# Seven gate and value groups ahead of a q transpose in TensorE's queue of a retention-plus-SwiGLU kernel

## The chip, the cores and the metric

The kernel runs on one core of a Trainium2 chip. A core has TensorE (matrix products, written to PSUM), VectorE, ScalarE and GpSimd, and SyncE, which only issues transfers; GpSimd issues transfers too, beside its own arithmetic. The metric is the device time of one execution in microseconds (us); lower is better. In the profile PE is TensorE's matmuls, PEld its weight loads, DVE is VectorE, ACT is ScalarE, POOL is GpSimd and SP is SyncE.

## What is computed

```python
def _attn_ref(q, k, v):                       # q, k, v: 4 x 8 x 768 x 64
    gamma = 1.0 - 2.0 ** (-5.0 - np.arange(H))
    for t in range(S):
        state = gamma * state + einsum('bhd,bhe->bhde', k[:, :, t], v[:, :, t])
        y[:, :, t] = scale * einsum('bhd,bhde->bhe', q[:, :, t], state)

def _moe_ref(x, w_gate, w_val, w_out, rms_g): # x: 3072 tokens x 512
    xn = x / sqrt(mean(x * x) + 1e-06) * rms_g
    g = xn @ w_gate                           # 512 x 1536
    return (g * sigmoid(g) * (xn @ w_val)) @ w_out
```

The first part is a linear attention with a decay per head; its output, token by token, goes through an RMS norm and a gated feed-forward network.

## The kernel before

**How the work is cut.** The 768 positions are cut into 6 chunks (c, 0 to 5) of 128, and there are 4 batches (b, 0 to 3), so a chunk has 4 x 128 = 512 tokens. Per chunk and batch the attention part transposes q and k, multiplies k with q to scores, masks the scores, multiplies them with v and adds the contribution of the state. Then come the norm, a transpose of the normed rows, and the feed-forward part, which works on the whole chunk: 12 blocks (n, 0 to 11) of 128 hidden columns for the gate and for the value. The output product, and in chunk 5 the gate and value products as well, are done with 7 products of sums and differences of quarters in place of 8; those sums are the z operations.

**What sets the order.** The order is written out by hand in a table, `ORDER` (lines 17 to 105), one word for each operation. A loop at the end (lines 784 to 788) takes the words one after the other and calls the function of that name; each engine runs what it is given strictly in that order, and waits where an operand or a buffer isn't ready:

```python
for w in ORDER.split():
    w, _, bk = w.partition("/")
    w, _, en = w.partition("@")
    f, *a = w.split(".")
    F[f](ENG.get(en), [int(i) for i in bk], *map(int, a))
```

A word is the operation's name, its numbers, after `@` the engine (D, A, P or S for VectorE, ScalarE, GpSimd or SyncE), and after `/` the PSUM banks that its result goes to. `g.0.4.6.3.4/4` is the gate product of chunk 0, blocks 4 to 5, batch 3, in bank 4. There are 8 banks, each with one buffer: a new result in a bank waits until the last reader of the former one is done. So the digit behind `/` orders engines too.

**The words that are spoken of:**

- `Lq`, `Lk`, `Lv` (line 329): load of q, k or v of chunk.batch; `wg`, `wv` (line 338) and `wo` (line 345): load of weight columns. On GpSimd's queue they convert to bf16 on the way; the tiles are `qb`, `kb`, `vp`, `wg_b`, `wv_b`, `wo_b`.
- `Tq`, `Tk` (line 386): transpose of q or k on TensorE into PSUM (`t_ps`), 4 matmuls. `Eq` (lines 395 and 152) and `Ek` copy the result to `qT` and `kT`. From chunk 2 on, `tq` and `tk` (line 402) do the transposes by DMA on SyncE's queue.
- `A` (line 418): scores (`a_ps`); `M0`, `M1` (line 441): masking on VectorE; `Y` (lines 456 and 460): scores times v, plus q times the state (`y_ps`).
- `K` (line 541), `U` (line 549), `B` (line 556): the state's update, its sum on VectorE, and on GpSimd the state in bf16 (`st_b`); `D` (line 532): k times its decay.
- `S` (line 473), `R` (lines 483 and 485), `N` (line 497): the row's sum of squares on ScalarE, `ms` and `rstd` on GpSimd (two instructions of 128x1), and the normed row `xn` on VectorE. `X` (line 510) transposes it, `XE` (line 152) copies it to `xnT`.
- `g`, `v` (line 564): gate and value product, 4 matmuls for each block; `s` (line 574): SiLU of the gate on ScalarE; `h` (line 586): its product with the value on VectorE, into `hT`.
- `z1` to `z4` (line 633): the sums of quarters of `hT` for the 7 products; `a1`, `b2`, `c5` and so on (line 660): those products.
- in chunk 5 `ga..`, `gb..`, `gc..`, `va..` and so on (line 750): its gate and value products; `gq`, `vq` (line 152) keep a part of them in SBUF (`sn`), `gr`, `vr` (line 762) add the parts, `gs` (line 772) is the SiLU.

A gate product of 4 matmuls reads the normed rows of the batches that its last two numbers span, so `g.0.4.6.3.4` needs batch 3 of chunk 0 only, `g.0.5.6.0.3` batches 0 to 2:

```python
for n in range(n0, n1):
    for s in range(KS):
        nc.tensor.matmul(p[:, (n - n0) * m:(n - n0 + 1) * m], W[w][0][:, s, n * 128:(n + 1) * 128],
                         xnT[c][:, s, b0 * C:b1 * C], start=s == 0, stop=s == KS - 1)
```

Of the kernel before, what the change touches and what calls it, by code (L numbers as in the profile page):

```python
# [23 lines left out]
K.0.2/2 S.0.3 s.0.0.2.0.1 N.0.1 U.0.2@A wg.4.6 X.0.2/5 R.0.3 XE.0.2@D D.0.1@D v.0.0.2.0.1/6 X.0.1/1 wv.4.6 causal
XE.0.1@A Lk.1.2@P v.0.0.2.2.3/4 h.0.0.2.0.1 g.0.0.2.2.3/2 D.0.3@D g.0.0.2.1.2/5 g.0.2.3.0.3/7 s.0.0.2.2.3 h.0.0.2.2.3
s.0.0.2.1.2 g.0.3.4.0.3/1 N.0.3 v.0.0.2.1.2/6 D.1.1@D s.0.3.4.0.3 Lq.1.2@P K.0.1/3 Tk.1.1/2 Ek.1.1@D K.0.3/5 X.0.3/4
h.0.0.2.1.2 Tq.1.2/0 Eq.1.2@D wg.6.9 v.0.3.4.0.3/1 Tq.1.1/2 Lk.1.3@P XE.0.3@A g.0.0.4.3.4/6 s.0.2.3.0.3 v.0.2.3.0.3/4
v.0.5.6.0.3/7 Eq.1.1@D Lq.1.3@P U.0.1@A U.0.3@A h.0.2.3.0.3 wv.6.9 g.0.5.6.0.3/3 s.0.5.6.0.3 g.0.4.5.0.3/5 Tk.1.2/2
h.0.3.4.0.3 h.0.5.6.0.3 v.0.4.5.0.3/4 Tk.1.3/0 v.0.4.6.3.4/1 v.0.0.4.3.4/3 s.0.4.5.0.3 h.0.4.5.0.3 Ek.1.2@A A.1.2/75
s.0.0.4.3.4 h.0.0.4.3.4 Ek.1.3@A g.0.7.8.0.4/2 s.0.7.8.0.4 g.0.4.6.3.4/4 s.0.4.6.3.4 Tq.1.3/6 g.0.6.7.0.4/0 mc.0@P  # L30
g.0.8.9.0.4/3 s.0.8.9.0.4 Lq.1.0@P mc.1@P Lk.1.0@P M0.1.2 Lv.1.3@P Eq.1.3@D h.0.4.6.3.4 Tq.1.0/7 M1.1.2 Eq.1.0@D
# [787 lines left out]
```

## Time and profile before

| | us |
|---|---|
| three runs | 232.84, 234.69, 234.11 (median 234.11) |
| the profiled execution, its own time | 233.33 |
| its span, first to last instruction | 231.6 (1.7 lies around it) |
| PE busy | 219.7 |
| DVE, POOL, ACT busy | 178.0, 151.0, 100.1 |

The profile shows one execution. A row of its timeline reads: start in us from the span's start, duration in us, engine, line, operation, out<-in, shapes, how many instructions; in square brackets how long the engine was idle before it, and what ended that. `PEclk` and the granted clock are the share of TensorE's full clock that it was given. Matmuls are pipelined: a group's next one starts before the last one's end is shown, so starts are compared with starts.

### The profile page before, as it was taken

To read this page: it belongs to the slowest core of one execution; us is meant where nothing else is said; L and a number is where in the kernel's file an instruction comes from. 1 tells how busy PE (TensorE), PEld (TensorE's weight loads), DVE (VectorE), ACT (ScalarE), POOL (GpSimd) and SP (SyncE) were. 2 spreads that over 40 slices of the span, in tenths; PEclk is the share of its full clock that TensorE was granted. 3 is DMA by queue.
4 is the path that set the end of the run, shared out by engine and by line. 5 is a ranking of instruction groups with operands and counts; after the bars stand their busy time and mean duration, and the time that the engine had idled before them with its cause. 6 is when DMAs were issued, how large, how long until landed. Compare 5 with 4: busy or idle time off the path is not lost.

```text
span 231.6 us, 5477 instructions
## 1 busy us (share of the span) xinstructions
PE 219.7 (95%) x2100; PEld 147.0 (63%) x2119; DVE 178.0 (77%) x328; ACT 100.1 (43%) x222; POOL 151.0 (65%) x207
## 2 busy tenths in 40 slices
PE   8999299999999999999999999999999999999992
PEld 3568177566445796446765446787446678888871
DVE  6598136986498978869768888889889589999931
ACT  7875224364436441332702454425442536863220
POOL 8969999738906862837814980377269789477700
PEclk9999889999999999999999999999999999999999
DMA  7999999998289967769758966955957353000243
GB/s 135 156 182 135 160 174 179 207 185 199 57 159 165 209 126 173 127 133 212 153 128 216 224 148 130 203 147 142 264 112 180 25 159 136 3 0 3 90 165 110
DMA packets 108172, 33.65 MB, mean 145 GB/s; under 512 B 94449, under 2 KB 108145, under 8 KB 108146
## 3 DMA queue, kind: packets, MB, share of 16 engines
q1 hardware_dynamic: 84674, 25.70, 49.3%
q0 software_dynamic: 23472, 7.60, 30.1%
q8 instruction: 16, 0.26, 0.5%
q14 instruction: 10, 0.08, 0.1%
HBM read 28.31 MB, written 6.29 MB: 149 GB/s over the span
## 4 chain that ended last, share of the span: by engine, by line
PE 85%; DMA 5%; POOL 4%; DVE 2%; issue 2%; ACT 1%; POOLq 0%; DVEq 0%
PE v_ps L564 22%; PE g_ps L564 21%; PE a L660 13%; PE c L660 7%; PE b L660 3%; DMA qb<-in_q_dram 2%; PE ga L750 2%; PE va L750 2%; DMA kb<-in_k_dram 2%; PE a_ps L418 2%; PE y_ps L456 2%; PE y_ps L460 2%; PE kv_ps L541 1%; PE vc L750 1%; PE gc L750 1%
## 5 line engine op out<-in xcount | busy, mean ns | idle before, releaser
L574 ACT ACTIVATE sg<-g_ps 128x512 bf16<-128x512 f32 (+2 forms) x64 | 35.5, 570 | 64.8 <-PE g_ps L564 52.4
L564 PE MATMUL v_ps<-xnT,wv_b 128*128 128x512 bf16 (+2 forms) x287 | 58.7, 340 | 0.6 <-issue 0.2
L564 PE MATMUL g_ps<-xnT,wg_b 128*128 128x512 bf16 (+2 forms) x286 | 57.9, 341 | 0.5
L586 DVE TENSOR_TENSOR hT<-sg,v_ps 128x512 bf16<-128x512 bf16 (+2 forms) x64 | 40.7, 649 | 15.8 <-PE v_ps L564 11.5
L564 PEld LDWEIGHTS <-wv_b 128*128 128x128 bf16 x296 | 26.0, 98 | 23.0 <-issue 0.3
L564 PEld LDWEIGHTS <-wg_b 128*128 128x128 bf16 x296 | 26.2, 100 | 22.3
L660 PEld LDWEIGHTS <-hT 128*128 128x128 bf16 x288 | 27.6, 98 | 4.6 <-issue 0.6
L633 POOL TENSOR_TENSOR z<-hT 128x512 bf16<-128x512 bf16 x10 | 12.3, 1234 | 19.1 <-DVE hT L586 18.9
L660 PEld LDWEIGHTS <-z 128*128 128x128 bf16 x216 | 20.6, 98 | 4.0 <-issue 0.7
L473 ACT ACTIVATE xsq<-y_ps 128x512 bf16<-128x512 f32 x22 | 13.2, 599 | 20.4 <-PE y_ps L460 17.3
L633 POOL TENSOR_TENSOR hT<-hT 128x512 bf16<-128x512 bf16 x12 | 15.2, 1265 | 10.1 <-DVE z L633 5.3
L441 DVE TENSOR_TENSOR am<-a_ps,causal 128x512 bf16<-128x512 f32 x32 | 20.1, 682 | 1.6 <-PE a_ps L418 1.4
L497 DVE SCALAR_TENSOR_TENSOR xn<-y_ps,rstd,g_bc 128x512 bf16<-128x512 f32 x22 | 16.4, 748 | 6.1 <-POOL rstd L485 6.1
L556 POOL CAST st_b<-st_f 64x256 bf16<-64x256 f32 x40 | 17.4, 434 | 1.9 <-DVE st_f L549 0.6
L660 PE MATMUL a<-wo_b,hT 128*128 128x256 bf16 x144 | 18.0, 273 | 0.0
L152 ACT COPY sn<-a 128x512 f32<-128x512 f32 x15 | 8.8, 586 | 15.4 <-PE a L660 13.1
L485 POOL TENSOR_TENSOR rstd<-ms,mhalf 128x1 f32<-128x1 f32 x24 | 13.2, 552 | 2.0
L683 DVE TENSOR_TENSOR r<-c,sn 128x512 f32<-128x512 f32 (+1 forms) x13 | 8.4, 647 | 7.1 <-PE c L660 4.4
L633 POOL TENSOR_TENSOR z<-z,hT 128x512 bf16<-128x512 bf16 x9 | 10.6, 1179 | 4.5 <-DVE z L633 3.1
L483 POOL TENSOR_SCALAR ms<-ssq 128x1 f32<-128x1 f32 x24 | 4.5, 189 | 12.8 <-ACT xsq L473 11.8
L549 DVE TENSOR_TENSOR st_f<-st_f,kv_ps 128x256 f32<-128x256 f32 x16 | 6.5, 416 | 5.0 <-PE kv_ps L541 5.0
L441 DVE TENSOR_TENSOR am<-a_ps,mask 128x512 bf16<-128x512 f32 x16 | 10.3, 683 | 0.0
(159 smaller groups left out, 393.8 us busy)
## 6 DMA issues: line engine op xcount, KB each, us to landing
out_dram<-r SPq DMA_DIRECT2D x22, 256.0 KB, 2.4
kf<-in_k_dram SPq DMA_DIRECT2D x18, 256.0 KB, 3.9
qf<-in_q_dram SPq DMA_DIRECT2D x16, 256.0 KB, 4.2
vf<-in_v_dram SPq DMA_DIRECT2D x16, 256.0 KB, 4.1
wo_b<-in_moe_w_out_dram POOLq DMA_DIRECT2D x3, 512.0 KB, 11.6
qb<-in_q_dram POOLq DMA_DIRECT2D x8, 128.0 KB, 5.3
vp<-in_v_dram POOLq DMA_DIRECT2D x8, 128.0 KB, 6.4
kb<-in_k_dram POOLq DMA_DIRECT2D x6, 128.0 KB, 5.3
```

The lines of the kernel that those rows point to most:

```text
L152: (e.copy if e is ACT else e.tensor_copy)(out, in_)
L441: DVE.tensor_tensor(out=u["am"][:, i], in0=u["a"][i], in1=m, op=ALU.mult)
L473: ACT.activation(xsq, flat(u["y"]), AF.Square, accum_out=u["ssq"])
L485: POOL.tensor_tensor(out=u["rstd"], in0=ms, in1=mhalf, op=ALU.pow)
L497: DVE.scalar_tensor_tensor(out=u["xn"], in0=flat(u["y"]), scalar=u["rstd"], in1=g_bc, op0=ALU.mult, op1=ALU.mult)
L556: POOL.tensor_copy(st_b[b][r, :, i * 64:i * 64 + 64], st_f[b][r])
L564: nc.tensor.matmul(p[:, (n - n0) * m:(n - n0 + 1) * m], W[w][0][:, s, n * 128:(n + 1) * 128], xnT[c][:, s, b0 * C:b1 * C], start=s == 0, s ...
L574: ACT.activation(sg[:, :cols], done["wg", c, n0, b0][:, :cols], AF.Silu)
L586: DVE.tensor_tensor(out=h_of(c, r)[:, i:i + n1 - n0, b0 * C:b1 * C], in0=sg, in1=p, op=ALU.mult)
L633: e.tensor_tensor(out=x, in0=a, in1=b, op=how)
L660: nc.tensor.matmul(done[x, c][:, q], left(i, c, r)[:, k, q * C:q * C + C], right(i)[:, r, k], start=first and q == r == k == 0, stop=r == ...
L750: nc.tensor.matmul(p[:, q], l[:, r, q], m[:, k], start=first and q == k == 0, stop=q == k == 1, skip_group_check=True)
```

## The change

Nothing is computed otherwise: the table holds the same 1065 words. What changes is where some stand, and the bank digits of most words that have one. Two lines of the table (before and after):

```diff
-h.0.0.2.1.2 Tq.1.2/0 Eq.1.2@D wg.6.9 v.0.3.4.0.3/1 Tq.1.1/2 Lk.1.3@P XE.0.3@A g.0.0.4.3.4/6 s.0.2.3.0.3 v.0.2.3.0.3/4
+K.0.3/7 X.0.3/5 h.0.0.2.1.2 wg.6.9 v.0.3.4.0.3/2 Tq.1.1/4 Lk.1.3@P XE.0.3@A g.0.0.4.3.4/0 g.0.4.6.3.4/3 v.0.2.3.0.3/1
```

**TensorE, end of chunk 0.** These rows are TensorE's from the transpose of batch 3's normed rows on (`xt_ps`); of each group of like matmuls the first is shown. Before, `t_ps_677` is `Tq.1.2`, the q transpose of chunk 1, batch 2, and `t_ps_690` is `Tq.1.1`:

```order
L510 MATMUL xt_ps_671<-ident_94,xn_629 128x128
L386 MATMUL t_ps_677<-ident_94,qb_644 128x128
L564 MATMUL v_ps_685<-xnT_496,wv_b_134 128x384
L386 MATMUL t_ps_690<-ident_94,qb_414 128x128
L564 MATMUL g_ps_698<-xnT_496,wg_b_133 128x128
L564 MATMUL v_ps_717<-xnT_496,wv_b_134 128x384
L564 MATMUL v_ps_722<-xnT_496,wv_b_134 128x384
L564 MATMUL g_ps_735<-xnT_496,wg_b_133 128x384
L564 MATMUL g_ps_742<-xnT_496,wg_b_133 128x384
L386 MATMUL t_ps_747<-ident_94,kb_581 128x128
L564 MATMUL v_ps_755<-xnT_496,wv_b_134 128x384
```

The same place after, where `t_ps_743` is `Tq.1.2`, `t_ps_685` is `Tq.1.1`, and `g_ps_710` is `g.0.4.6.3.4`:

```order
L510 MATMUL xt_ps_673<-ident_94,xn_629 128x128
L564 MATMUL v_ps_680<-xnT_496,wv_b_134 128x384
L386 MATMUL t_ps_685<-ident_94,qb_414 128x128
L564 MATMUL g_ps_693<-xnT_496,wg_b_133 128x128
L564 MATMUL g_ps_710<-xnT_496,wg_b_133 128x128
L564 MATMUL v_ps_719<-xnT_496,wv_b_134 128x384
L564 MATMUL v_ps_724<-xnT_496,wv_b_134 128x384
L564 MATMUL g_ps_730<-xnT_496,wg_b_133 128x384
L564 MATMUL g_ps_736<-xnT_496,wg_b_133 128x384
L386 MATMUL t_ps_743<-ident_94,qb_646 128x128
L386 MATMUL t_ps_757<-ident_94,kb_581 128x128
```

`Tq.1.2` moved from the first place behind `X.0.3` to behind seven gate and value groups and `Tq.1.1`; six of those seven already stood next to it, and `g.0.4.6.3.4` comes up from behind the first scores of chunk 1 (`A.1.2`). A little further on `Tk.1.3` moves behind `v.0.4.6.3.4` and `v.0.0.4.3.4`. ScalarE's and VectorE's copies and products follow: `s.0.2.3.0.3` goes ahead of the copy `XE.0.3`, and on VectorE `h.0.3.4.0.3` and `h.0.2.3.0.3` go ahead of `Eq.1.1` and `Eq.1.2`. GpSimd's loads stay as they were.

**GpSimd, chunk 1.** One piece of the difference of GpSimd's queue; the kd rows ahead of it are `D.1.0` and `D.1.2`, z is `z1.0.0`, st_b_127 is the state of batch 2 (`B.0.2`), and the first ms and rstd rows are `R.1.3`:

```order
 L532 TENSOR_TENSOR kd<-kb,vdec 128x512 x2
-L633 TENSOR_TENSOR z<-hT 128x512
-L556 CAST st_b_127<-st_f_123 64x4x64 x2
 L483 TENSOR_SCALAR ms<-ssq 128x1
 L485 TENSOR_TENSOR rstd<-ms,mhalf 128x1
+L556 CAST st_b_127<-st_f_123 64x4x64 x2
+L633 TENSOR_TENSOR z<-hT 128x512
```

`R.1.3` moves ahead of `B.0.2` and `z1.0.0`, and these two change places; `R.1.1`, `R.1.0` and `R.1.2` follow behind as before.

**VectorE, chunk 5.** TensorE's order in chunk 5 is unchanged, VectorE's and ScalarE's is not. VectorE before, from `gr3.5.1` (vf_3528) on; `vf_3546` is `vr2.5.1`, z_3576 is `z1.4.0`, `vf_3582` is `gr3.5.0`, and the row that reads `va_3438` is `h.5.6.8.0.2`:

```order
L762 TENSOR_TENSOR vf_3528<-gc_3481,sn_3405 128x512
L762 TENSOR_TENSOR vf_3546<-vc_3533,sn_3544 128x512
L586 TENSOR_TENSOR hT_3522<-kb_3505,vf_3546 128x2x256
L633 TENSOR_TENSOR z_3576<-hT_3250 128x512
L762 TENSOR_TENSOR vf_3582<-gc_3515,sn_3496 128x512
L586 TENSOR_TENSOR hT_3522<-kb_3511,va_3438 128x2x256
L762 TENSOR_TENSOR vf_3604<-vc_3533,sn_3502 128x512
```

And after, with `vr2.5.1` as vf_3585 and `gr3.5.0` as vf_3592:

```order
L762 TENSOR_TENSOR vf_3528<-gc_3481,sn_3405 128x512
L633 TENSOR_TENSOR z_3567<-hT_3250 128x512
L586 TENSOR_TENSOR hT_3520<-kb_3522,va_3438 128x2x256
L762 TENSOR_TENSOR vf_3585<-vc_3531,sn_3542 128x512
L586 TENSOR_TENSOR hT_3520<-kb_3505,vf_3585 128x2x256
L762 TENSOR_TENSOR vf_3592<-gc_3513,sn_3496 128x512
L762 TENSOR_TENSOR vf_3626<-vc_3531,sn_3502 128x512
```

`h.5.6.8.0.2` moves ahead of three operations that stood before it, and `vr3.5.1` (vf_3604, now vf_3626) stays behind `gr3.5.0`.

**Banks.** Of the 255 words that take banks, 108 now follow another word in their bank than before. Two that are used below: `Tk.1.2` (t_ps_757) now follows `Tq.1.2` in bank 4, and `vb2.5.2` in chunk 5 now follows `va1.5.1` in bank 3, the accumulator that `h.5.6.8.0.2` reads last.

More of the change, by code (lines that the diff above doesn't have):

```diff
@@ L94 @@
-gq7.5.0@D gc5.5.0/5 gr2.5.0 h.5.4.6.0.2 gc3.5.1 gr3.5.1 gs2.5.0 s4.3@S vc5.5.1/7 vS3.0@P vS3.1@P va7.5.1 vq7.5.1@A
-vr2.5.1 h.5.6.8.2.4 va6.5.0 vq6.5.0@A ga4.5.0 gs4.5.0 a1.4.0.3/1 gq6.5.2@A z1.4.0@D gc3.5.0 gr3.5.0 va4.5.1 va1.5.2/4
-gs3.5.1 h.5.6.8.0.2 vq1.5.2@A vS4.0@P vc3.5.1 vr3.5.1 z2.4.0@P h.5.4.6.2.4 vb2.5.2/3 gs3.5.0 va7.5.0 vq7.5.0@A
-vc5.5.0/5 ga7.5.2 va6.5.2 vr2.5.0 vr1.5.2 gc5.5.2/6 gq7.5.2@A gr2.5.2 q1.4@A z4.4.1@P vq6.5.2@A h.5.8.10.0.2
-b2.4.0.3/7 vc3.5.0 ga4.5.2 h.5.2.4.2.4 gc3.5.2 vr3.5.0 gs2.5.2 s3.3@S s2.3@S z1.5.1@D z3.4.2@P va4.5.0 va7.5.2
@@ L99 @@
[L99 to L103 removed]
+Ek.0.1@A Ek.0.2@D yd Lk.0.3@P H.1/4 Tq.0.2/3 tab Lq.0.3@P Eq.0.2@D hot.2/6 A.0.0/7502 M0.0.0 G/1 M1.0.0 Tq.0.3/4
@@ new lines @@
+gr1.5.1 ga6.5.1 gq6.5.1@D va1.5.0/4 gq1.5.0@A gb2.5.0/6 gr1.5.0 gs1.5.1 ga1.5.2/7 gq1.5.2@A gS3.0@P vq1.5.0@D
+gb2.5.2/0 va1.5.1/3 gs1.5.0 vq1.5.1@A gr1.5.2 vb2.5.0/5 gs1.5.2 z2.4.2@P vr1.5.0 ga7.5.1 ga6.5.0 vb2.5.1/6 h.5.0.2.0.2
+ga6.5.2 vr1.5.1 gc5.5.1/0 X4.5@P va6.5.1 gq7.5.1@A gr2.5.1 gq6.5.0@A ga7.5.0 vq6.5.1@A s2.2@S gs2.5.1 ga4.5.1
+gq7.5.0@D gc5.5.0/5 gr2.5.0 h.5.4.6.0.2 gs4.5.1 gc3.5.1 gr3.5.1 s4.3@S vc5.5.1/6 vS3.0@P vS3.1@P va7.5.1 vq7.5.1@A
+va6.5.0 vq6.5.0@A ga4.5.0 a1.4.0.3/2 z1.4.0@D gc3.5.0 va4.5.1 va1.5.2/0 h.5.6.8.0.2 gs2.5.0 vr2.5.1 h.5.6.8.2.4
@@ new lines @@
+gs4.5.0 gq6.5.2@A gr3.5.0 vq1.5.2@A vS4.0@P vc3.5.1 z2.4.0@P vb2.5.2/3 va7.5.0 vc5.5.0/1 ga7.5.2 va6.5.2 vr3.5.1
+vq7.5.0@A vr2.5.0 gc5.5.2/5 gq7.5.2@A z4.4.1@P b2.4.0.3/6 vc3.5.0 ga4.5.2 h.5.2.4.2.4 gs3.5.1 h.5.4.6.2.4 gs3.5.0
+vr1.5.2 gr2.5.2 q1.4@A vq6.5.2@A h.5.8.10.0.2 gc3.5.2 vr3.5.0 gs2.5.2 s3.3@S s2.3@S z1.5.1@D z3.4.2@P va4.5.0 va7.5.2
+h.5.0.2.2.4 z4.4.0@P z1.5.0@P z2.5.0@P z4.4.2@P h.5.2.4.0.2 vc5.5.2/3 gr3.5.2 a6.4.0.3 a1.5.0.2/1 z3.4.0@D vq7.5.2@A
+vr2.5.2 h.5.10.12.2.4 s2.1@S va4.5.2 z3.5.0@P q6.4@A gs4.5.2 h.5.10.12.0.2 b2.5.0.2/4 gs3.5.2 a1.5.2.3 vc3.5.2
```

148 lines of the change are left out of this document (71 added, 77 removed).

## The prediction

> **What bounds the kernel now.** I read first the page, then TensorE's waits, its timeline about the longest of them, and the granted clock there. The page says that TensorE is nearly always busy, except in two of the early slices:
>
> ```profile
> span 231.6 us, 5477 instructions
> PE   8999299999999999999999999999999999999992
> PEclk9999889999999999999999999999999999999999
> ```
>
> TensorE's longest wait over the whole span (us in total, times, longest); the next one is 1.1 us at the start:
>
> ```profile
> PE t_ps L386 <- DMA qb<-in_q_dram: 4.2, 1, 4.2
> ```
>
> TensorE's timeline there: the transpose that waits is `Tq.1.2`, behind `X.0.3`, and the groups that follow it are `v.0.3.4.0.3`, `Tq.1.1` and `g.0.0.4.3.4`; the last two rows, `Tq.1.0` and `Tk.1.0`, are used further on.
>
> ```profile
> 22.86 0.40 PE L510 MATMUL xt_ps<-ident,xn 128*128 128x128 bf16 x4
> 27.47 0.61 PE L386 MATMUL t_ps<-ident,qb 128*128 128x128 bf16 x4 [4.21 <-DMA qb<-in_q_dram]
> 27.87 1.49 PE L564 MATMUL v_ps<-xnT,wv_b 128*128 128x384 bf16 x4
> 29.15 0.63 PE L386 MATMUL t_ps<-ident,qb 128*128 128x128 bf16 x4
> 29.57 1.61 PE L564 MATMUL g_ps<-xnT,wg_b 128*128 128x128 bf16 x16
> ...
> 39.76 0.39 PE L386 MATMUL t_ps<-ident,qb 128*128 128x128 bf16 x4
> 39.98 0.39 PE L386 MATMUL t_ps<-ident,kb 128*128 128x128 bf16 x4
> ```
>
> In windows cut at the clock's steps (us, then busy time of PE, PEld, DVE, ACT, POOL, each with its count, then the granted clock) the idle stretch is followed by 3.41 us at half clock. The last row, of the long stretch behind, says that TensorE is then busy for 191.5 of 193.0 us: whatever comes earlier at 31 us should come earlier at the end too.
>
> ```profile
> 23.90:27.32 3.42, 0.00 (x0) 0.00 (x0) 0.00 (x0) 0.92 (x3) 3.42 (x5) 1.00 1.78 156
> 27.32:30.73 3.41, 3.26 (x23) 2.59 (x24) 1.38 (x2) 0.00 (x0) 3.39 (x4) 0.50 1.81 171
> ...
> 31.00:224.00 193.00, 191.51 (x1725) 128.55 (x1742) 157.23 (x264) 81.26 (x177) 122.93 (x158) 1.00 0.72 144
> ```
>
> **The change part by part.**
>
> *The q transpose behind seven groups.* The wait of 4.21 us ends because TensorE now has work: `v.0.3.4.0.3` can start when the transposes of 22.86 have been issued. The half clock goes with it: the 3.26 us of work in that window are 1.63 us at full clock. Together 5.84 us, the gross gain, if nothing else is late.
>
> What is late next is the queue of GpSimd's loads. Its order and its issues don't change, so I take its landings as fixed. Three rows for the walk that follows: eight matmuls of 384 columns at full clock in the chain (start, us), ScalarE's copy `XE.0.3`, and VectorE's copy `Eq.1.2`:
>
> ```profile
> 32.49 1.30 PE g_ps L564 x8
> ...
> 23.30 0.58 ACT L152 COPY xnT<-xt_ps 128x512 bf16<-128x512 bf16 x1 [1.10 <-PE xt_ps L510]
> ...
> 28.11 0.69 DVE L395 TENSOR_TENSOR qT<-t_ps,qdec 128x512 bf16<-128x512 bf16 x1 [4.64 <-PE t_ps L386]
> ```
>
> So a group of 4 x 384 columns takes 0.65, and by its columns one of 16 x 128 takes 0.87 and four transposes 0.22. Counted from 23.1 at full clock: `v.0.3.4.0.3` to 23.75, `Tq.1.1` to 24.0, `g.0.0.4.3.4` (its rows are copied to `xnT` by 23.9) to 24.8, `g.0.4.6.3.4` to 25.3, the four groups of 0.65 to 27.9. Only then comes `Tq.1.2`, whose q landed at 27.42: no wait. `Tk.1.2` now uses the same bank, so it waits for the copy `Eq.1.2`, 0.69 us on VectorE: to about 29.0, some 0.75 us of TensorE. From there the groups go on to 34.5, where `Tq.1.0` needs a q and then `Tk.1.0` a k. These two loads, GpSimd's issues with their time to landing:
>
> ```profile
> L329 POOL DMA_DIRECT2D qb<-in_q_dram x1: 955/955/955, 27.2 to 27.2; - x1
> DMA to landing us min/median/max: 7.8/7.8/7.8
> ...
> L329 POOL DMA_DIRECT2D kb<-in_k_dram x1: 948/948/948, 29.1 to 29.1; - x1
> DMA to landing us min/median/max: 6.7/6.7/6.7
> ```
>
> They land at 27.18 + 7.76 = 34.94 and 29.14 + 6.70 = 35.84 (the rows round the first digits away). So `Tk.1.0` starts at 35.9 instead of 39.98: a lead of 4.1 us. Of the gross 5.84 about 1.75 go to these waits, the 0.75 at the bank among them.
>
> *GpSimd's row sum ahead of the gate sum.* GpSimd's own rows, and the two of TensorE that wait for its results (`Y.1.2`'s second half, which needs `B.0.2`, and `X.1.1` with `X.1.0`):
>
> ```profile
> 40.27 2.04 POOL L532 TENSOR_TENSOR kd<-kb,vdec 128x512 bf16<-128x512 bf16 x2
> 42.27 1.14 POOL L633 TENSOR_TENSOR z<-hT 128x512 bf16<-128x512 bf16 x1
> 43.37 0.84 POOL L556 CAST st_b<-st_f 64x256 bf16<-64x256 f32 x2
> 45.46 0.19 POOL L483 TENSOR_SCALAR ms<-ssq 128x1 f32<-128x1 f32 x1 [1.25 <-ACT xsq L473]
> 45.73 0.56 POOL L485 TENSOR_TENSOR rstd<-ms,mhalf 128x1 f32<-128x1 f32 x1
> ...
> 48.05 0.39 PE L460 MATMUL y_ps<-st_b,qT 128*128 128x128 bf16 x4
> ...
> 51.09 0.61 PE L510 MATMUL xt_ps<-ident,xn 128*128 128x128 bf16 x8
> ```
>
> GpSimd doesn't wait for anything up to 42.27, so it can't come earlier there. With TensorE 4.1 us ahead the sum of squares for `R.1.3` is ready by 41.4 and GpSimd starts it at 42.27: 0.83 for `R.1.3`, 0.84 for `B.0.2` (to 43.95; `Y.1.2`'s second half starts there instead of at 48.05), 1.1 for `z1.0.0`, twice 0.8 for `R.1.1` and `R.1.0` (to 46.6), then the normed row, 0.75 on VectorE, to 47.35. `X.1.0` starts there instead of at 51.31 (0.22 behind 51.09): the lead is 3.95. So this part caps the lead, and takes 0.15 more. If `z1.0.0` had stayed first, `R.1.3` would have come 1.1 later, the gain of the move; with no lead the move is worth nothing, since GpSimd waited anyway.
>
> *VectorE's and ScalarE's order in chunk 5.* VectorE's and TensorE's rows of before (`vr2.5.1`, `h.5.6.8.0.2`; `va4.5.1`, `vb2.5.2`; then the transfer of the lag, `z2.5.2` on GpSimd and `a6.5.2.3` on TensorE):
>
> ```profile
> 200.37 0.68 DVE L762 TENSOR_TENSOR vf<-vc,sn 128x512 f32<-128x512 f32 x1
> 202.63 0.68 DVE L586 TENSOR_TENSOR hT<-kb,va 128x512 bf16<-128x512 bf16 x1
> ...
> 201.73 0.60 PE L750 MATMUL va<-qb,wv_b 128*128 128x256 bf16 x4
> 203.04 0.60 PE L750 MATMUL vb<-xnT,wv_b 128*128 128x256 bf16 x4
> ...
> 216.46 1.15 POOL L633 TENSOR_TENSOR z<-z,hT 128x512 bf16<-128x512 bf16 x1 [1.18 <-PE c L660]
> 217.89 0.60 PE L660 MATMUL a<-w,z 128*128 128x256 bf16 x4
> ```
>
> `h.5.6.8.0.2` needs `va4.5.1`, whose end is 201.73 + 0.60 = 202.33. VectorE does `z1.4.0` at 200.4 and then idles to 202.35, where before it did three other operations: 1.6 us of idle. It frees bank 3 at 203.0, just as `vb2.5.2` wants it. Behind it VectorE is 1.1 us late at 209 and, having had waits of its own, some 0.5 late at 216. `z2.5.2` then ends at 217.6 + 0.5, and `a6.5.2.3` waits 0.2. The bounds are 0 (cover holds) and 1.6 (the whole idle time passes to the end); I take 0.2, the row that is nearest, since TensorE's other needs there (banks 1, 5 and 6) are met 0.2 us or more ahead.
>
> *Banks.* For each of the 108 new neighbours I looked for when the last reader was done in the rows of before: none is late except where the order has moved as well, which the walk above contains. I set 0, with 0.2 either way for the least distances.
>
> *Loads of chunk 2.* SyncE's first loads wait for weights to land and don't move. The load of the q that GpSimd scales first (`Cq.2.0`), the time to landing of the loads of q about it, and GpSimd's scaling:
>
> ```profile
> 49.63 1.40 SPq L329 DMA_DIRECT2D qf<-in_q_dram  x1
> ...
> DMA to landing us min/median/max: 3.4/4.0/4.3
> ...
> 59.70 1.04 POOL L354 TENSOR_TENSOR qb<-qf,ydec 128x512 bf16<-128x512 f32 x1
> ```
>
> It is there by 49.63 + 4.3 = 53.9 and is wanted at 59.7, or at 55.75 with the lead: 1.8 us of cover remain.
>
> **The sum**, for the profiled execution: 233.33 - 4.21 - 1.63 + 1.75 + 0.15 + 0.2 = 229.6. That execution was 0.78 below the median of the three runs; from 234.11 the same 3.74 us give 230.4. I predict 230.2, between the two and nearer to the median.
>
> **Rivals.**
>
> *The half clock isn't in the timed runs.* An idle stretch of 4.2 us and a clock that steps each 3.41 us: here a whole step, 23.90 to 27.32, was empty. Were the steps shifted by more than 0.8 us against the kernel, no step would be empty. Then before has no 1.63 to lose, and the gain is 3.74 - 1.63 = 2.1: 232.0. For it: only one profiled execution shows the clock. Against: it isn't slower than the others, and a lone execution without the cost should have been below 232. [...]
>
> *GpSimd is slowed by VectorE's earlier work.* VectorE was idle from 23.5 to 28.1, while GpSimd issued loads; now it works there. If each VectorE operation kept GpSimd waiting, the 3.8 us of work that comes under GpSimd's busy stretch would delay its whole chain by up to 3.8, and with it `X.1.0`: 234.0, no change. GpSimd's issues of two loads of weights speak against it, with the window of the first beside them (VectorE, the third pair, busy for 0.76; in the second's, within 23.90 to 27.32 above, for nothing):
>
> ```profile
> 20.10 0.81 POOL L338 DMA_DIRECT2D wv_b<-in_moe_w_val_dram  x1
> 25.42 0.80 POOL L338 DMA_DIRECT2D wv_b<-in_moe_w_val_dram  x1
> ...
> 20.10:20.91 0.81, 0.81 (x10) 0.55 (x8) 0.76 (x3) 0.63 (x2) 0.81 (x2) 1.00 0.92 101
> ```
>
> The issue takes 0.81 with VectorE busy and 0.80 with it idle. [...]
>
> *The wait only moves.* TensorE meets the next load. If the loads from 30 us on landed 2 us later than in this trace, the lead at `Tk.1.0` would be 2.1: 232.2; 4 us later, nothing would be left: 234. The queue's evenness speaks against it (34.94, 35.84).
>
> *The tail takes it.* All of VectorE's 1.6 us pass to the end: 231.6.
>
> *Slower.* The new waits (0.75, 0.5, 0.7) keep the clock down: each window of 3.41 us at half clock costs 1.7. TensorE has 1.9 us of slack to `Tk.1.0`, so it takes four such windows in a row, 6.8, before the lead is gone (34.0 + 6.8 against 39.98): then some 235.0. The clock stayed at 1.00 in all windows without an idle stretch of their own length, which speaks against it.
>
> **How the numbers follow.** The forecast has 0.70; the clock rival 0.10, GpSimd's lock 0.03, the moved wait 0.06, the tail 0.07, slower 0.04. A measurement of this kernel tells about 1% from no change, 231.8 and 236.5 here. Faster: 0.70, half of the clock's and the tail's, together 0.79. Same: the rest of these, the lock, the moved wait and a quarter of slower, whose 235.0 is within 1% until a fifth window adds 1.7: 0.18. Slower 0.03. The forecast's own range is 229.2 (no cost in the tail, from the profiled execution, 4.1 of gain) to 231.4; with the scatter of the runs below and the clock and tail rivals above, 228.9 to 232.5.
>
> **What would show it.** Right: no wait of TensorE over 1 us before 30; the granted clock at 1.00 from 23.9 to 31; `Tk.1.0` at 35.9 waiting for its load; GpSimd's `R.1.3` at 42.3 without a wait; `X.1.0` at 47.4; VectorE idle for 1.6 us before `h.5.6.8.0.2`; span near 227.9. Wrong: `Tk.1.0` later than 36.5 (the loads or GpSimd's issues are later), a window at half clock, or TensorE idle in chunk 5.

## The result, and the profile after

The changed kernel takes 235.20 us (median of 20 runs, 233.73 to 236.41), the kernel before 234.13 (median of 20, 232.51 to 237.05). The ratio is 1.0054, with a 95% interval of 1.0029 to 1.0079: half a per cent slower, where 230.2 had been forecast. Ratios, here and below, leave out executions over 1.5% above the fastest of their kernel, such as the 237.05, so they differ a little from the quotient of the medians. The profiled execution took 235.53 us itself. Its page, the three lines that answer to those of before (span, TensorE's busy tenths in 40 slices, its clock):

```profile
span 233.8 us, 5480 instructions
PE   7999899999998999999999999999999999769992
PEclk9999999999999999999999999999999999988998
```

The light slice near the start, the fifth, is gone, as forecast. There are two others now, the 35th and 36th (199 to 210 us), and the clock is down in the 36th and 37th (205 to 216 us). So the gain arrives early and is lost late.

**Early, the walk holds but for its last step.** TensorE's timeline from `X.0.3` on (start, us, and in brackets the idle time ahead):

```profile
22.33 0.40 PE L510 MATMUL xt_ps<-ident,xn 128*128 128x128 bf16 x4
22.57 0.81 PE L564 MATMUL v_ps<-xnT,wv_b 128*128 128x384 bf16 x4
...
27.38 0.39 PE L386 MATMUL t_ps<-ident,qb 128*128 128x128 bf16 x4
28.55 0.38 PE L386 MATMUL t_ps<-ident,kb 128*128 128x128 bf16 x4 [0.78 <-DVE qT L395]
...
34.97 0.40 PE L386 MATMUL t_ps<-ident,kb 128*128 128x128 bf16 x4 [0.35 <-DMA kb<-in_k_dram]
```

`Tq.1.2` (27.38) doesn't wait. `Tk.1.2` waits 0.78 for the bank, and `Tk.1.0` starts at 34.97 behind its load, where it started at 39.98. This execution runs some 0.5 us ahead before the change of order begins (`X.0.3` at 22.33 against 22.86), so 4.5 of the 5.0 us belong to the change. The 0.5 is luck: the same three matmuls (`hot_ps`) take 0.81 us at 4.83 here and 1.49 us at 5.00 in before's profiled execution, and another execution of the same program (e7 below) has `X.0.3` at 22.91. GpSimd's `R.1.3` follows without a wait, and TensorE's `Y.1.2` (second half) and `X.1.0`:

```profile
41.77 0.19 POOL L483 TENSOR_SCALAR ms<-ssq 128x1 f32<-128x1 f32 x1
```

```profile
43.47 0.38 PE L460 MATMUL y_ps<-st_b,qT 128*128 128x128 bf16 x4 [0.26 <-POOL st_b L556]
...
47.54 0.40 PE L510 MATMUL xt_ps<-ident,xn 128*128 128x128 bf16 x4 [0.51 <-DVE xn L497]
```

`X.1.0` stands at 47.54 instead of 51.31, a lead of 3.8 us; without the 0.5 it is 3.3.

**Late, the lead goes.** TensorE in chunk 5: `va4.5.1`, `va1.5.2`, `vc3.5.1`, then `va6.5.2`, `b2.4.0.3`, `ga4.5.2`, `gc3.5.2`, and at the end `a1.5.0.2`:

```profile
198.15 0.60 PE L750 MATMUL va<-qb,wv_b 128*128 128x256 bf16 x4
198.59 0.60 PE L750 MATMUL va<-xnT,wv_b 128*128 128x256 bf16 x4
200.20 0.60 PE L750 MATMUL vc<-xnT,kf 128*128 128x256 bf16 x4 [1.01 <-DVE vf L762]
...
202.66 0.60 PE L750 MATMUL va<-qb,vf 128*128 128x256 bf16 x4
...
204.00 1.47 PE L660 MATMUL b<-wo_b,hT 128*128 128x256 bf16 x12 [0.30 <-DVE vf L762]
...
205.96 0.60 PE L750 MATMUL ga<-qb,wg_b 128*128 128x256 bf16 x4
208.41 0.84 PE L750 MATMUL gc<-xnT,kf 128*128 128x256 bf16 x4 [1.86 <-DVE vf L762]
...
213.13 1.04 PE L660 MATMUL a<-wo_b,hT 128*128 128x256 bf16 x8
```

`va4.5.1` starts at 198.15, before at 201.73: the lead is still 3.58. A group of four takes 0.44 from start to start (`b2.4.0.3`, with twelve, 1.31), so each start shows what was lost ahead of it: `vc3.5.1` 1.17, `va6.5.2` 0.27, `b2.4.0.3` 0.47, `ga4.5.2` 0.2, `gc3.5.2` 2.0. Together 4.1: at `gc3.5.2` the kernel is 0.56 us behind before, where that product started at 207.85. Then comes a step at half clock (us, busy time of PE, PEld, DVE, ACT, POOL, clock):

```profile
205.20:208.62 3.42, 1.54 (x13) 1.06 (x11) 2.93 (x6) 2.39 (x5) 0.00 (x0) 1.00 0.00 0
208.62:212.03 3.41, 3.41 (x19) 2.42 (x16) 3.41 (x8) 1.52 (x3) 1.32 (x2) 0.50 0.00 0
```

It costs another 1.7: `a1.5.0.2` starts at 213.13, in the kernel before it was at 210.90. The two rows of before, `gc3.5.2` and `a1.5.0.2`:

```profile
207.85 0.60 PE L750 MATMUL gc<-xnT,kf 128*128 128x256 bf16 x4
...
210.90 1.04 PE L660 MATMUL a<-wo_b,hT 128*128 128x256 bf16 x8
```

That is 3.58 + 2.23 = 5.8 us lost in 15 us, and the 2.2 us by which the spans differ.

**Who is waited for.** VectorE's rows there are `z1.4.0`, `h.5.6.8.0.2`, `vr2.5.1`, then `gr3.5.0`, `vr3.5.1`, `vr2.5.0`, then `h.5.4.6.2.4` and `gr2.5.2`:

```profile
196.79 0.42 DVE L633 TENSOR_TENSOR z<-hT 128x512 bf16<-128x512 bf16 x1
198.86 0.69 DVE L586 TENSOR_TENSOR hT<-kb,va 128x512 bf16<-128x512 bf16 x1 [1.65 <-PE va L750]
199.47 0.68 DVE L762 TENSOR_TENSOR vf<-vc,sn 128x512 f32<-128x512 f32 x1
...
201.24 0.69 DVE L762 TENSOR_TENSOR vf<-gc,sn 128x512 f32<-128x512 f32 x1
203.25 0.69 DVE L762 TENSOR_TENSOR vf<-vc,sn 128x512 f32<-128x512 f32 x1 [1.32 <-PE va L750]
204.59 0.69 DVE L762 TENSOR_TENSOR vf<-vc,sn 128x512 f32<-128x512 f32 x1 [0.65 <-ACT sn L152]
...
206.47 0.69 DVE L586 TENSOR_TENSOR hT<-kb,vf 128x512 bf16<-128x512 bf16 x1 [0.46 <-ACT kb L772]
...
207.68 0.68 DVE L762 TENSOR_TENSOR vf<-gc,sn 128x512 f32<-128x512 f32 x1
```

ScalarE's rows are the SiLU `gs2.5.0`, then `vq1.5.2`, `vq7.5.0`, `gq7.5.2`, and the SiLUs `gs3.5.1` and `gs3.5.0` as one row:

```profile
197.45 0.63 ACT L772 ACTIVATE kb<-vf 128x512 bf16<-128x512 f32 x1
...
202.02 0.58 ACT L152 COPY sn<-va 128x512 f32<-128x512 f32 x1 [1.25 <-DVE vf L762]
203.98 0.58 ACT L152 COPY sn<-va 128x512 f32<-128x512 f32 x1 [1.37 <-DVE vf L762]
205.32 0.58 ACT L152 COPY sn<-ga 128x512 f32<-128x512 f32 x1 [0.76 <-DVE vf L762]
205.80 1.15 ACT L772 ACTIVATE kb<-vf 128x512 bf16<-128x512 f32 x2
```

Read them as a relay. VectorE's idle 1.65 us is the 1.6 of the prediction. What had not been seen is who stands behind it: `vr2.5.1` now comes after it (199.47 to 200.15), and `vc3.5.1` adds into the very bank that `vr2.5.1` reads, so TensorE starts it at 200.20. Then the three engines wait for each other in turn: `gr3.5.0` (to 201.93), ScalarE's `vq1.5.2` at 202.02, TensorE's `va6.5.2` at 202.66 (it adds into the bank that `vq1.5.2` copies), VectorE's `vr3.5.1` at 203.25, ScalarE's `vq7.5.0` at 203.98, VectorE's `vr2.5.0` at 204.59, ScalarE's `gq7.5.2` at 205.32 and behind it `gs3.5.1`, VectorE's `h.5.4.6.2.4` at 206.47, and last `gr2.5.2` (to 208.36), for which `gc3.5.2` waits.

### The profile page after: what moved, and what is told of

Read it like the earlier page. It is cut to its first block, busy times and chain, and to the rows that moved or that the text cites. A ratio compares the mean times of both kernels' runs of the same rounds, so it can differ in the third digit from the quotient of the medians.

```text
span 233.8 us, 5480 instructions
## 1 busy us (share of the span) xinstructions
PE 220.1 (94%) x2100; PEld 146.4 (63%) x2119; DVE 178.8 (76%) x328; ACT 100.6 (43%) x222; POOL 151.2 (65%) x207
## 4 chain that ended last, share of the span: by engine, by line
PE 69%; POOL 12%; DVE 8%; ACT 4%; issue 3%; DMA 2%; DVEq 0%; ACTq 0%; POOLq 0%
PE g_ps L564 15%; PE v_ps L564 15%; PE a L660 13%; PE c L660 7%; PE b L660 3%; DVE hT L586 2%; PE va L750 2%; DMA kb<-in_k_dram 2%; PE a_ps L418 2%; PE ga L750 2%; PE y_ps L456 2%; DVE vf L762 2%; POOL vp L329 2%; PE y_ps L460 1%; PE kv_ps L541 1%
## 5 line engine op out<-in xcount | busy, mean ns | idle before, releaser
L564 PE MATMUL v_ps<-xnT,wv_b 128*128 128x512 bf16 (+2 forms) x287 | 57.7, 338 | 0.6 <-issue 0.2
L564 PE MATMUL g_ps<-xnT,wg_b 128*128 128x512 bf16 (+2 forms) x286 | 57.2, 337 | 0.6 <-issue 0.2
L564 PEld LDWEIGHTS <-wg_b 128*128 128x128 bf16 x296 | 25.5, 98 | 22.1
L660 PEld LDWEIGHTS <-hT 128*128 128x128 bf16 x288 | 27.6, 98 | 5.1 <-issue 1.1
L633 POOL TENSOR_TENSOR hT<-hT 128x512 bf16<-128x512 bf16 x12 | 14.5, 1210 | 9.4 <-DVE z L633 4.7
```

Of the source, the lines that this page charges most:

```text
L633: e.tensor_tensor(out=x, in0=a, in1=b, op=how)
L660: nc.tensor.matmul(done[x, c][:, q], left(i, c, r)[:, k, q * C:q * C + C], right(i)[:, r, k], start=first and q == r == k == 0, stop=r == ...
```

## The experiments

Theory A was that the new order of VectorE and ScalarE in chunk 5 loses the lead; the rivals were the new banks there (B), and an end that doesn't come earlier with TensorE whatever the order is (C). Each ratio is to the kernel before, timed beside the run (medians 234.54 us for e1 to e4, 233.87 for e5 to e8, 233.78 for e9 to e12); across these groups ratios are compared, not times.

### Words and banks of chunk 5, together and apart

**e1**: the changed kernel with chunk 5 from `ga4.5.1` on as before; the diff shows the part that moves most, and the six words whose bank differs are `vb2.5.2`, `vc5.5.0`, `gc5.5.2`, `vc5.5.2`, `a1.5.0.2` and `c5.4.0.3`.

```diff
-gr2.5.0 h.5.4.6.0.2 gs4.5.1 gc3.5.1 gr3.5.1 ... vq7.5.1@A va6.5.0 vq6.5.0@A ga4.5.0 a1.4.0.3/2 z1.4.0@D ... h.5.6.8.0.2 gs2.5.0 vr2.5.1 h.5.6.8.2.4
+gs4.5.1 ... gr2.5.0 h.5.4.6.0.2 gc3.5.1 gr3.5.1 gs2.5.0 ... vq7.5.1@A vr2.5.1 h.5.6.8.2.4 va6.5.0 vq6.5.0@A ... z1.4.0@D ... gs3.5.1 h.5.6.8.0.2
```

> The changed kernel with everything of chunk 5 from ga4.5.1 on put back as it was before the change: the order of the words, and the six banks that differ (renamed to fit). In the changed kernel's trace TensorE is 3.58 us ahead of before up to 199 us and loses it behind that. Theory A (the new order of VectorE and ScalarE in chunk 5 loses it) and theory B (the six new banks there lose it) both expect the lead to reach the end: 234.1 - 3.6 = 230.5 us, ratio to before 0.985. Theory C (the end hangs on something that doesn't come earlier with TensorE, so that any lead is lost there) expects 234 us and TensorE's waits near 200 us again. If the half clock near 27 us isn't in the timed runs of before, the ratio is 0.991 (2.1 us).

Measured: 231.20 us, ratio to before 0.9866 (0.9819 to 0.9913). The lead reaches the end, so theory C falls. The profiled execution, of 232.82 us, had two steps at half clock near its start (the third slice; before the change of order begins):

```profile
PEclk9959999999999999999999999999999999999998
```

**e2**: the old order, with the new banks for the six words (the diff of e1, less the bank digits).

> The changed kernel with the old order of words from ga4.5.1 on, but with the new banks for the six words. Theory A: as fast as with both put back, 230.5 us, no wait of TensorE above 0.5 us between 195 and 215 us. Theory B: as slow as the changed kernel, 235.2 us. If both count, between the two.

Measured: 230.70 us, ratio 0.9856 (0.9828 to 0.9884). The span, and TensorE's one wait in the gate and value products of chunk 5:

```profile
span 228.8 us, 5500 instructions
PE vb L750 <- DVE hT L586: 0.2, 1, 0.2
```

**e3**: the new order, with the old banks.

```diff
-vb2.5.2/3 ... vc5.5.0/1 ... gc5.5.2/5 ... vc5.5.2/3 ... a1.5.0.2/1 ... c5.4.0.3/5
+vb2.5.2/1 ... vc5.5.0/5 ... gc5.5.2/3 ... vc5.5.2/1 ... a1.5.0.2/5 ... c5.4.0.3/3
```

> The changed kernel with its new order, and the old banks for the six words of chunk 5. Theory A: as slow as the changed kernel, 235.2 us, with the waits of 1.0 us (vc3.5.1) and 1.9 us (gc3.5.2) still there. Theory B: 230.5 us and no such waits. The wait of 0.3 us at b2.4.0.3 should stay by both, since that word's bank is the same in both.

Measured: 235.10 us, ratio 1.0052 (1.0026 to 1.0078), as the changed kernel. TensorE's waits for VectorE are all there (the second row now counts two):

```profile
PE gc L750 <- DVE vf L762: 1.9, 1, 1.9
PE vc L750 <- DVE vf L762: 1.3, 2, 1.0
```

The order is the cause and the six banks are not. With the old banks the new order has 1.0052 against 0.9866 (e1), with the new banks 1.0054 (the changed kernel) against 0.9856 (e2): 2%, 4.4 and 4.6 us.

**e4**: before, with the new chunk 5 alone (the reverse of e1's diff, in the kernel before).

> The kernel before with only chunk 5's part of the change (new order and new banks from ga4.5.1 on); the early part isn't made. Theories A and B: the tail costs what it costs in the changed kernel, 1.17 + 0.27 + 0.46 + 0.21 + 2.1 = 4.2 us at full clock, some 1.6 more where a stretch at half clock follows: 238.3 to 240 us, ratio 1.018 to 1.025. Theory C: without a lead there is nothing to lose, 234 to 235 us.

Measured: 237.42 us, ratio 1.0146 (1.0107 to 1.0186), which is 3.4 us and less than theories A and B had. The same two waits stand in a kernel without a lead, beside the old wait for q, so the tail costs by itself and doesn't merely eat a lead:

```profile
PE t_ps L386 <- DMA qb<-in_q_dram: 3.9, 1, 3.9
PE gc L750 <- DVE vf L762: 1.9, 1, 1.9
...
PE vc L750 <- DVE vf L762: 1.0, 1, 1.0
```

### Which part of the order

Here the question was whether the losses in chunk 5 add up (D), hang on the first one (E), or on the last one (F).

**e5**: one pair put back on VectorE.

```diff
-z1.4.0@D gc3.5.0 va4.5.1 va1.5.2/0 h.5.6.8.0.2 gs2.5.0 vr2.5.1 h.5.6.8.2.4
+vr2.5.1 h.5.6.8.2.4 z1.4.0@D gc3.5.0 va4.5.1 va1.5.2/0 h.5.6.8.0.2 gs2.5.0
```

> The changed kernel; on VectorE vr2.5.1 and h.5.6.8.2.4 stand ahead of z1.4.0 again, nothing else is put back. Theory D (a chain: VectorE's idle 1.65 us in front of h.5.6.8.0.2 delays vr2.5.1, for which vc3.5.1 on TensorE waits 1.0, and what comes behind is a second, separate loss): the waits of 1.0 at vc3.5.1 and of 0.27 at va6.5.2 go, the 1.9 at gc3.5.2 stays, 235.2 - 1.4 = 233.8 us. Rival E (one late operation at the head of the chain is the whole loss): everything behind comes earlier too, 230.7 us. Rival F (gc3.5.2 is the only thing that counts, TensorE just waits there longer): 235.2.

Measured: 234.70 us, ratio 1.0030 (0.9998 to 1.0063): a quarter of a per cent below the changed kernel's, and the intervals overlap. The wait at `vc3.5.1` went, and another of 0.9 came at `vb2.5.2`, whose bank `h.5.6.8.0.2` reads; `vr2.5.1`, though moved up, waited for a SiLU on ScalarE:

```profile
PE vb L750 <- DVE hT L586: 0.9, 1, 0.9
```

```profile
199.41 0.69 DVE L762 TENSOR_TENSOR vf<-vc,sn 128x512 f32<-128x512 f32 x1 [1.24 <-ACT kb L772]
```

By its number this is nearest to F, but not by its rows: the first loss was replaced by another, which the rows of the changed kernel had hidden. D's and E's numbers are both missed.

**e6**: the other end of the chain. Two SiLUs, `gs3.5.1` and `gs3.5.0`, move up on ScalarE with it, so VectorE's order isn't the only change.

```diff
-vq1.5.2@A ... h.5.2.4.2.4 gs3.5.1 h.5.4.6.2.4 gs3.5.0 vr1.5.2 gr2.5.2
+vq1.5.2@A gs3.5.1 gs3.5.0 ... vr1.5.2 gr2.5.2 h.5.2.4.2.4 h.5.4.6.2.4
```

> The changed kernel; on VectorE vr1.5.2 and gr2.5.2 stand ahead of h.5.2.4.2.4 and h.5.4.6.2.4 again, and for that gs3.5.1 and gs3.5.0 on ScalarE ahead of vq7.5.0 (their results have to be read before the two get buffers). Theory D: vr2.5.0 still starts at 204.6, vr1.5.2 at 205.2, gr2.5.2 at 205.9, so gc3.5.2 starts at 206.65 instead of 208.41: 1.75 us, and as much as 1 us more where the stretch at half clock behind it goes too: 232.5 to 233.5 us. Rival E: no change, 235.2. Rival F: nearly all, 230.7.

Measured: 233.76 us, ratio 0.9993 (0.9965 to 1.0021): 0.6% or 1.4 us better than the changed kernel. The 1.9 at `gc3.5.2` is gone, a wait of 0.6 for `z2.5.2` at `a6.5.2.3` is new; the 1.0 at `vc3.5.1` stayed. D had 1.7 to 2.7, so this is nearest to D and below it.

**e7**: one word written earlier in the table, with no engine's order changed.

```diff
-vc3.5.1 z2.4.0@P vb2.5.2/3 va7.5.0 vc5.5.0/1 ga7.5.2 va6.5.2 vr3.5.1
+vc3.5.1 vr3.5.1 z2.4.0@P vb2.5.2/3 va7.5.0 vc5.5.0/1 ga7.5.2 va6.5.2
```

> The changed kernel with the word vr3.5.1 written directly behind vc3.5.1, as before the change. Each engine's order stays the same; only the buffer that its result gets is another, since buffers are given out in the order of the table. Theory D: vr3.5.1 waits 1.32 us for va6.5.2 because it got the buffer of the sum of weights that va6.5.2 is the last to read; without it VectorE goes on at 201.85 and gc3.5.2 starts at 207.0 instead of 208.41: 1.4 us, with the clock up to 1 more: 233 to 233.8 us. Rival G (the wait is for the product vc3.5.1 itself, or hidden behind the next one): no change, 235.2, and the wait of 1.3 us ahead of vr3.5.1 is still there.

Measured: 234.81 us, ratio 1.0054 (1.0024 to 1.0083), the changed kernel again, and `vr3.5.1` still waits:

```profile
203.84 0.69 DVE L762 TENSOR_TENSOR vf<-vc,sn 128x512 f32<-128x512 f32 x1 [1.32 <-PE va L750]
```

So the word's own place doesn't choose its buffer; I had that wrong. Built, the table of e7 gives the program of the changed kernel: the same instructions in the same order on every engine, with the same buffers. The run is a second measurement of the changed kernel and doesn't decide between D and G. In both programs `vr3.5.1` takes over the buffer of a sum of weights that `va6.5.2` is the last to read, although that word stands behind it in e7's table. In the kernel before, and in e9 below, it takes over the buffer of `gr3.5.1`'s sum, which the SiLU `gs3.5.1` is the last to read. So what decides is the place of the reader that frees a buffer, and this gave the next theory.

**e8**: the three edits together.

```diff
-z1.4.0@D ... h.5.6.8.0.2 gs2.5.0 vr2.5.1 h.5.6.8.2.4 ... vq1.5.2@A ... va6.5.2 vr3.5.1 ... h.5.2.4.2.4 gs3.5.1 h.5.4.6.2.4 gs3.5.0 vr1.5.2 gr2.5.2
+vr2.5.1 h.5.6.8.2.4 z1.4.0@D ... h.5.6.8.0.2 gs2.5.0 ... vq1.5.2@A gs3.5.1 gs3.5.0 ... vc3.5.1 vr3.5.1 ... vr1.5.2 gr2.5.2 h.5.2.4.2.4 h.5.4.6.2.4
```

> The changed kernel with the three edits together (vr2.5.1 ahead, vr1.5.2 and gr2.5.2 ahead, vr3.5.1 behind vc3.5.1); h.5.6.8.0.2, h.5.4.6.2.4 and GpSimd stay as changed. Theory D: no wait of TensorE over 0.4 us behind 195 us, and the time of the old order: 230.7 us, within 0.7. If something else in the new order costs, it lies between this and 235.2.

Measured: 232.86 us, ratio 0.9946 (0.9922 to 0.9970). Half of the loss is back, not all of it: two waits are left that the changed kernel doesn't show.

```profile
PE vb L750 <- DVE hT L586: 0.9, 1, 0.9
PE a L660 <- POOL z L633: 0.6, 1, 0.6
```

### ScalarE's share

Theory H came from e5 and e7: besides VectorE's own order, three SiLUs that moved back on ScalarE (`gs2.5.0`, `gs3.5.1`, `gs3.5.0`) hold buffers that VectorE writes next.

**e9**: the changed kernel, ScalarE's order put back.

```diff
-vq7.5.1@A ... vq6.5.0@A ... gs2.5.0 ... gq6.5.2@A ... vq1.5.2@A ... gq7.5.2@A ... gs3.5.1 ... gs3.5.0
+gs2.5.0 vq7.5.1@A ... vq6.5.0@A ... gq6.5.2@A ... gs3.5.1 vq1.5.2@A gs3.5.0 ... gq7.5.2@A
```

> The changed kernel with ScalarE's order in chunk 5 put back (the SiLU gs2.5.0 ahead of vq7.5.1, gs3.5.1 and gs3.5.0 ahead of and behind vq1.5.2); VectorE's and TensorE's orders stay as changed. Theory H (the late SiLUs hold buffers that VectorE writes next: with gs3.5.1 late, vr3.5.1 has to take the buffer that va6.5.2 reads, and waits 1.3 us; VectorE's own order costs the rest): the wait at vr3.5.1 goes, gc3.5.2 starts near 206.9 instead of 208.4, the 1.0 us at vc3.5.1 stays: 235.1 - 1.5, and up to 1 more with the clock: 232.6 to 233.6 us. Rival (VectorE's order alone counts): 235.1.

Measured: 232.63 us, ratio 0.9952 (0.9932 to 0.9972), 1% or 2.4 us better than the changed kernel with neither VectorE's nor TensorE's order touched. `vr3.5.1` follows `gr3.5.0` without a wait, and on TensorE `vc3.5.1` still waits 1.0, `gc3.5.2` now 1.0 instead of 1.9:

```profile
202.25 0.68 DVE L762 TENSOR_TENSOR vf<-vc,sn 128x512 f32<-128x512 f32 x1
```

```profile
200.59 0.60 PE L750 MATMUL vc<-xnT,kf 128*128 128x256 bf16 x4 [1.01 <-DVE vf L762]
...
207.31 0.60 PE L750 MATMUL gc<-xnT,kf 128*128 128x256 bf16 x4 [1.04 <-DVE vf L762]
```

**e10**: the good kernel (e2) with one SiLU late.

```diff
-gs2.5.0 ... vq7.5.1@A vr2.5.1 h.5.6.8.2.4 va6.5.0 vq6.5.0@A
+vq7.5.1@A vr2.5.1 h.5.6.8.2.4 va6.5.0 vq6.5.0@A gs2.5.0
```

> The kernel with the old order of words in chunk 5 (230.7 us) and one SiLU moved: gs2.5.0 stands behind vq7.5.1 and vq6.5.0 on ScalarE, as in the changed kernel. VectorE's order is the old one. Theory H: vr2.5.1 is given the buffer that gs2.5.0 reads and waits some 1.2 us for it; VectorE is as late at h.5.6.8.0.2, and vb2.5.2 on TensorE, in that row's bank, waits about 1.5 us: 232.2. Rival (ScalarE has room, its order is harmless): 230.7, no wait of VectorE over 0.5 us ahead of vr2.5.1.

Measured: 231.77 us, ratio 0.9910 (0.9882 to 0.9938), against 0.9856 for e2: 1.3 us, though the two intervals touch. The profiled executions have the same: `va4.5.1` starts at 198.63 (e2: 198.65) and `a1.5.0.2` at 209.46 (e2: 208.13). VectorE's `vr2.5.1` waits for the SiLU, and TensorE's `vb2.5.2` for `h.5.6.8.0.2`:

```profile
198.60 0.69 DVE L762 TENSOR_TENSOR vf<-vc,sn 128x512 f32<-128x512 f32 x1 [1.24 <-ACT kb L772]
```

```profile
201.60 0.60 PE L750 MATMUL vb<-xnT,wv_b 128*128 128x256 bf16 x4 [1.49 <-DVE hT L586]
```

One instruction of 0.63 us, moved back by two places on an engine that is busy for 43% of the span, costs 1.3 us at the end. Both waits are where H had them, and of its size. The counterpart of e9 (VectorE's old order with all three SiLUs late) was not tried, so VectorE's own share is not shown apart.

### The early part

**e11**: e2, with `z1.0.0` still later on GpSimd.

```diff
-B.0.2 z1.0.0@P Y.1.2/5 N.1.3 ... z2.0.0@D R.1.1 ... R.1.0 ... N.1.0 X.1.1/3
+B.0.2 Y.1.2/5 N.1.3 ... R.1.1 ... R.1.0 z1.0.0@P ... N.1.0 z2.0.0@D X.1.1/3
```

> The kernel with the old order of words in chunk 5 (230.7 us), and on GpSimd z1.0.0 moved further back, behind R.1.1 and R.1.0 (z2.0.0 on VectorE behind N.1.0). If GpSimd's row sums cap the lead, as the prediction has it, R.1.0 comes 1.1 us earlier, the wait of 0.5 us at X.1.0 goes, and the time is 230.2 us. If not, 230.7.

Measured: 230.83 us, ratio 0.9885 (0.9843 to 0.9927): no gain that these runs can tell. The wait at `X.1.0` went, and `X.1.2` waits 0.33 in its place:

```profile
49.46 0.40 PE L510 MATMUL xt_ps<-ident,xn 128*128 128x128 bf16 x4 [0.33 <-DVE xn L497]
```

**e12**: e2, with GpSimd's order as before the change, so that the lead is made and GpSimd isn't adapted to it.

```diff
-D.1.2@P R.1.3 ... B.0.2 z1.0.0@P Y.1.2/5 N.1.3
+D.1.2@P z1.0.0@P ... B.0.2 Y.1.2/5 R.1.3 N.1.3
```

> The kernel with the old order of words in chunk 5 (230.7 us), and GpSimd's order as before the change: z1.0.0 and B.0.2 ahead of R.1.3. Theory (the move of R.1.3 is worth as much as it saves GpSimd ahead of it, now that TensorE leads): X.1.3 waits for N.1.3, some 1.4 us, Y.1.2's second half 0.3 us longer, and the 0.5 at X.1.0 goes: 231.9 us. Rival (hidden either way): 230.7.

Measured: 231.28 us, ratio 0.9900 (0.9867 to 0.9933), 1.0 us behind e2, though the two intervals overlap. `X.1.3` waits as expected:

```profile
46.62 0.40 PE L510 MATMUL xt_ps<-ident,xn 128*128 128x128 bf16 x4 [1.33 <-DVE xn L497]
```

## Why the prediction was wrong

**The q transpose: right.** The wait of 4.2 us and its half clock are gone (the granted clock is 1.00 from 23.0 to 31.0), the wait of 0.75 at the bank measured 0.78, and `Tk.1.0` waits for its load, which landed earlier than taken: the lead there is 4.5 us, not 4.1. That the half clock might not be in the timed runs can be dropped. The 17 executions of before that were timed beside e2 had a mean clock of at most 0.993 over the span, those of e2 0.993 to 1.000, and a step of 3.41 us at half clock lowers the mean by 3.41 x 0.5 / 232 = 0.007. By this estimate each of before lost at least one such step; where it lay the mean doesn't tell.

**GpSimd's row sum: right in kind, 0.65 us too good in size.** `R.1.3` starts without a wait right behind the kd rows, and GpSimd caps the lead (`X.1.0` waits 0.51 for the normed row). But the forecast 3.95 measured 3.3: the start of `X.1.0` fits the forecast (47.54 against 47.4) only by the head start of 0.5. In e2's profiled execution, which has next to none (`X.0.3` at 22.80), `R.1.3` starts at 42.26 and `X.1.0` at 48.02. From one to the other the walk has 5.1 us, the rows of both executions 5.8. With the order of before the gain is some 1.0 us smaller (e12), near the 1.1 of the prediction. With the tail of before the two early parts give 230.70 (e2), 3.4 us of the 3.9 that the sum has without its tail term.

**Banks: right as far as tested.** With the order as before, the old and new banks of the six words in chunk 5 give 0.9866 and 0.9856. The other new neighbours were not tried apart.

**GpSimd kept waiting by VectorE (the "lock" of the chances): it didn't come.** No run shows a lock between the two. VectorE is busy for 1.71 us from 23.0 to 27.6, where it was for 0.48 before, and the five instructions that GpSimd starts there (the issues of loads of k, q, `wv` and q, and one product for `mask`) take 0.91, 0.91, 0.80, 0.95 and 1.11 us, before 0.91, 0.91, 0.80, 0.95 and 1.10. `R.1.3` isn't later for it (41.77, without a wait). The operations that moved there are `h` and `Eq`; of others these runs say nothing.

**VectorE's and ScalarE's order in chunk 5: this step failed.** It was set at 0.2 us, with 0 and 1.6 as its bounds, "since TensorE's other needs there (banks 1, 5 and 6) are met 0.2 us or more ahead". It costs 4.1 us at full clock in the profiled execution, 5.8 with the step at half clock, and 2% or 4.4 to 4.6 us in the timed runs (e3 against e1, the changed kernel against e2). Three things were missed:

- *Bank 6 wasn't met.* The walk looked for new results in a bank. `vc3.5.1` is none: it adds to a result that `vr2.5.1` must have read before. `vr2.5.1` had moved behind the idle time, and ended at 200.15 where TensorE could have started at 199.03. And `b2.4.0.3`, the new result in bank 6, waits 0.30 for `vr3.5.1`. Idle time of VectorE isn't the price of a late operation; what is queued behind it is.
- *ScalarE was named in the heading and not walked.* Three SiLUs moved back there. Little hangs on their results (`h.5.4.6.2.4` waits 0.46 for one), but they are the last readers of buffers in SBUF into which VectorE writes its next sums (the six of `vf`), and ScalarE's copies wait for buffers (`sn`) that VectorE reads. Restoring ScalarE's order alone brings back half (e9); delaying one SiLU alone costs 1.3 us (e10).
- *The upper bound assumed one loss.* 1.6 was VectorE's idle time, taken once. In a ring of three engines that hold four or six buffers for each other the delay returned at `va6.5.2`, `b2.4.0.3`, `ga4.5.2` and `gc3.5.2`.

Removing single waits didn't remove their sum (e5, e6, e8), because the next one behind each came out. The remainder between e9 and e2, some 1%, is VectorE's order only by what is left (the 1.0 at `vc3.5.1` and at `gc3.5.2`); no run shows it alone. Of the signs that the prediction named for being wrong, "a window at half clock, or TensorE idle in chunk 5", both came, and both there.

**The best version** is e2: both early parts, with chunk 5's order as it was, 0.9856 (0.9828 to 0.9884) of before. The intervals of e1 and e11 overlap with it.

## What to carry to other kernels

When an order table moves words on an engine that isn't the bottleneck, list for every moved word which buffer its end sets free, in PSUM and in SBUF, and who takes it next; the results alone don't tell. Two products that add into a bank waited here for the reader of the sum so far, though no bank digit had changed (1.0 us at `vc3.5.1`, 1.9 at `gc3.5.2`). And a gain at the start should be tried with the tail left alone: e2 against the full change separates the two at once.

## What the runs showed of the hardware

The prediction had seen the clock fall only behind a step of 3.41 us in which TensorE stood still. In the changed kernel it fell behind one in which TensorE was busy for 1.54 us of 3.42 (the rows of 205.20 and 208.62 above). In e7, which is the same program, the edge of a step cuts the wait of 1.9 us at `gc3.5.2` in two, and the clock stayed at full. The place of its steps is an estimate, counted back in whole steps from the fall at the end; in the changed kernel's trace the clock changes at 208.62, 212.03 and 232.52, which are one and six steps of 3.41 apart. The rows of e7:

```profile
204.31:207.72 3.41, 2.53 (x20) 1.94 (x20) 2.27 (x5) 2.22 (x4) 0.00 (x0) 1.00 0.00 0
207.72:211.13 3.41, 2.14 (x20) 1.91 (x20) 3.41 (x8) 2.28 (x4) 0.00 (x0) 1.00 0.00 0
```

How much work keeps the clock up is not shown. In e12 it stayed behind a step with 1.81 us of 3.41 busy (28.34 to 31.75). In e1 it fell behind one with 2.59 us of 3.42, near the start, where TensorE does short transposes between waits for loads:

```profile
8.02:11.44 3.42, 2.59 (x57) 1.61 (x53) 2.03 (x5) 2.89 (x5) 3.42 (x5) 1.00 1.78 160
11.44:14.85 3.41, 3.41 (x52) 1.99 (x51) 2.23 (x5) 2.24 (x6) 1.61 (x3) 0.50 1.95 176
```

So the busy time of the matmuls doesn't decide alone. Whether the waits fall into one step or are cut by its edge differs between the profiled executions of the changed kernel and of e7, one program: a step's edge lies 1.95 us behind the start of `vr3.5.1` in the first (205.20 and 203.25), and 0.47 us behind it in the second (204.31 and 203.84). Of the 20 of the changed kernel, eight had a mean clock of 0.990 or 0.991 and took 235.5 to 236.4 us, eleven had 0.995 or more and took 233.7 to 235.3. That the two groups come from the place of the steps is an estimate: a step at half clock lowers the mean by 0.007, and the one in the profiled execution cost 1.7 us.
